# V in 8 KB runs, two batches interleaved over the partitions, and all weights loaded in pairs of slots: a decode kernel of two attention and two GLU layers

## The chip, the cores and the metric

The kernel runs on one core of a Trainium2 chip. The metric is the device time of one execution in microseconds (us). Before the change it is 189 us. With one core there are no others to compare a run with, so runs are called fast unless they lie over 1.5% above the fastest of their kernel. In the profiles PE is TensorE (matrix multiplication) and PEld its loading of weights, DVE VectorE, ACT ScalarE, POOL GpSimd; SPq is the queue of the SyncEngine, which issues all loads here; L372 is a line of the kernel; a landing is the moment at which a load is complete.

## The reference

Four layers in turn (attention, GLU, attention, GLU with the same weights), one new token for each of four batches, bf16.

```python
def attention(x, k_cache, v_cache, wq, wo):      # x: 4 x 1 x 512
    W = 2048                                      # the last 2048 of 8192 keys
    q = (x @ wq)                                  # 32 query heads of 128; 8 kv heads, each shared by 4
    scores = q . k[:, :, -W:, :] * 128 ** -0.5
    o = softmax(scores) . v[:, :, -W:, :]
    return o @ wo                                 # 4096 -> 512
def glu(x, w_gate, w_up, w_down):                 # 512 -> 1792 -> 512
    return (sigmoid(x @ w_gate) * (x @ w_up)) @ w_down

x = x + attention(layernorm(x), ...)
x = x + glu(layernorm(x), ...)
x = x + attention(layernorm(x), ...)
x = x + glu(layernorm(x), ...)
```

There is almost no arithmetic per byte. K and V windows are 16.8 MB each, `wq` and `wo` 4.2 MB each, the three GLU weights 5.5 MB together.

## The kernel before

SBUF holds one arena of 50 slots of 512 KB (4 KB on each of 128 partitions). K takes 32 slots and stays, transposed in place, for both attentions. The other 18 slots are a pool through which everything else streams, in one fixed order, from one load queue (the SyncEngine). `wo` stays after its first load. So do the last three V slots (`KEEP_V`), which the second attention, going through the heads backwards, uses first. Everything else is loaded twice.

V is one load of 512 KB per batch and head, 16 keys (4 KB, contiguous in memory) on a partition:

```python
def kv_d(cache, b, h):
    return cache[b, h, SK - W:SK, :].rearrange("(p j) d -> p (j d)", p=128)

def load_kv(name, cache, b, h):
    loads.append((name, lambda s: dma(str(name), slot_ap(s), kv_d(cache, b, h), w=[("slot", s)])))
# [cut] load_cols: 512 KB of wq, 448 KB of w_gate or w_up; load_rows: 512 KB of wo or w_down
```

A slot goes back to the pool when its last reader is emitted, and the next load in order is put on the queue with a wait on that reader:

```python
def done(name):
    pool.release(where.pop(name))
# [cut]
for gi, (h, b) in enumerate(pairs):               # P.V of one head: 4 batches
    s = need(("V", h, b))
    # [cut] 16 matmuls with 128 x 128 weights taken from the slot
    if (h, b) not in keep:
        done(("V", h, b))
        fill()
```

P leaves softmax with the keys in the free dimension; a matmul with a permutation matrix and a 32 x 32 block transpose turn the keys onto the partitions:

```python
P.op("tensor", "pp" + tag, ..., lambda pe: pe.matmul(ps[:, PB, :], perm[:, :], prow[:, :], start=True, stop=True), ...)
P.op("scalar", "pc" + tag, ...)   # copy back to SBUF
P.op("vector", "pt" + tag, ...)   # 32 x 32 blocks transposed
```

## Time and profile before

| | before |
|---|---|
| time, median | 188.96 us at first, 189.06 us with the run beside the changed kernel |
| span of the profiled run | 187.5 us |
| bytes loaded | 72.37 MB in 122 loads |
| free slots while GLU 1 starts | 7 (18 less 8 of `wo` and 3 of V) |

First some lines of the page: the busy share of the DMA engines and what they moved in 40 equal slices, the count of packets, the head of the chain of waits, and the loads of V and K (count, KB each, median us from issue to landing).

```profile
span 187.5 us, 4426 instructions
...
DMA  4999999999999999999999999999999999999990
GB/s 167 421 421 428 425 407 396 426 383 418 404 395 425 384 415 408 397 421 393 396 402 385 410 408 337 368 410 395 409 408 407 405 409 406 407 409 404 405 371 11
DMA packets 20532, 72.65 MB, mean 387 GB/s; under 512 B 1944, under 2 KB 6048, under 8 KB 17952
...
DMA 38%; SPq 28%; PE 19%; DVE 7%; ACT 3%; issue 3%; ACTq 0%
...
arena<-in_A_v_cache_dram SPq DMA_DIRECT2D x61, 512.0 KB, 14.8
arena<-in_A_k_cache_dram SPq DMA_DIRECT2D x16, 1024.0 KB, 14.8
```

The DMA engines are full from the second slice to the last but one (9 tenths or more in each). What counts is how fast bytes pass, and whether the queue ever runs thin: see 337 and 368 in slices 25 and 26. The stretches view gives the same by time. Its last three columns are the TensorE clock granted, the mean busy share of the 16 DMA engines (packet durations over 16 x the stretch), and GB/s.

```profile
core 0: us, PE busy (x) PEld busy (x) DVE busy (x) ACT busy (x) POOL busy (x), PEclk, DMA share, GB/s
...
20.00:25.00 5.00, 2.02 (x16) 0.38 (x16) 4.91 (x6) 0.20 (x1) 0.00 (x0) 1.00 1.01 423
110.00:115.00 5.00, 3.08 (x26) 0.99 (x26) 1.35 (x6) 1.03 (x5) 0.00 (x0) 0.50 1.00 382
115.00:120.00 5.00, 1.85 (x30) 0.86 (x31) 0.86 (x2) 0.13 (x1) 0.00 (x0) 0.50 0.98 329
120.00:125.00 5.00, 2.07 (x46) 1.76 (x47) 1.26 (x8) 0.41 (x2) 0.00 (x0) 0.50 1.03 411
...
145.00:150.00 5.00, 4.69 (x116) 3.03 (x113) 2.08 (x8) 2.16 (x7) 0.76 (x4) 1.00 1.03 406
155.00:160.00 5.00, 4.71 (x103) 2.82 (x108) 1.82 (x6) 1.68 (x4) 1.13 (x6) 1.00 1.02 406
180.00:185.00 5.00, 2.64 (x63) 2.02 (x60) 1.04 (x3) 0.00 (x0) 0.00 (x0) 0.50 0.52 205
```

At 20 to 25 us only 8 KB packets (K) flow, at 145 to 160 us only 4 KB packets (V).

The waits of the load queue (for whom, us in total, times, longest) show the thin place. The queue stood 7.7 us before GLU 1's first matmuls (L845) gave slots back:

```profile
SPq L372 <- PE ps L755: 18.7, 13, 2.7
SPq L372 <- DVE prow L943: 14.3, 1, 14.3
SPq L372 <- PE ps L845: 9.8, 6, 7.7
```

### The profile page before, as it was taken

Reading aid. Unit: us, or ns where it says so; the run is one execution under the profiler, and the core shown is the slowest. Engines: PE = TensorE matmul, PEld = TensorE weight load, DVE = VectorE, ACT = ScalarE, POOL = GpSimd, SP = SyncE. Lnnn points to the kernel's source line nnn. Section 1 sums busy time; section 2 is a strip of 40 time slices with the busy share of each in tenths; the row PEclk is TensorE's granted clock in tenths of the full one; section 3 lists DMA queues with packets and bytes.
Section 4 is the critical chain, followed back from the end, with each engine's and each line's share of the span. In section 5 each row is a group of like instructions: output and inputs, shape, how many; then the busy total and the mean of one; then the engine's idle time right before and its main releaser. Section 6 shows DMA issues by size and latency. Waiting matters only on the chain.

```text
span 187.5 us, 4426 instructions
## 1 busy us (share of the span) xinstructions
PE 97.6 (52%) x1906; PEld 56.1 (30%) x1920; DVE 86.3 (46%) x215; ACT 32.7 (17%) x95; POOL 13.9 (7%) x73
## 2 busy tenths in 40 slices
PE   0532405456517163270734446344999999775643
PEld 0101002312404033040334331311255555474222
DVE  6109999267583755738510031122484443321211
ACT  2000021213303003020020001000363333210110
POOL 3000000101101001010010000000021111110000
PEclk9999996667857555576675555555799969955555
DMA  4999999999999999999999999999999999999990
GB/s 167 421 421 428 425 407 396 426 383 418 404 395 425 384 415 408 397 421 393 396 402 385 410 408 337 368 410 395 409 408 407 405 409 406 407 409 404 405 371 11
DMA packets 20532, 72.65 MB, mean 387 GB/s; under 512 B 1944, under 2 KB 6048, under 8 KB 17952
## 3 DMA queue, kind: packets, MB, share of 16 engines
q1 hardware_dynamic: 20512, 72.37, 97.9%
q8 instruction: 15, 0.25, 0.5%
q14 instruction: 5, 0.04, 0.1%
HBM read 72.36 MB, written 0.00 MB: 386 GB/s over the span
## 4 chain that ended last, share of the span: by engine, by line
DMA 38%; SPq 28%; PE 19%; DVE 7%; ACT 3%; issue 3%; ACTq 0%
SPq L372 28%; DMA arena<-in_A_k_cache_dram 16%; DMA arena<-in_B_w_down_dram 11%; PE ps L689 11%; DMA arena<-in_A_v_cache_dram 6%; DMA arena<-in_A_wq_dram 5%; PE ps L755 4%; DVE arena L669 3%; ACT prow L706 2%; DVE nmax L697 2%; ACT qbd L656 1%; PE ps L785 1%; PE ps L845 1%; PE ps L877 1%; DVE qbd L653 1%
## 5 line engine op out<-in xcount | busy, mean ns | idle before, releaser
L689 PE MATMUL ps<-arena,qbd 128*16 128x512 bf16 x256 | 32.3, 632 | 29.0 <-DVE arena L669 21.6
L755 PE MATMUL ps<-ebuf,arena 128*128 128x4 bf16 x1024 | 32.0, 166 | 14.9 <-DMA arena<-in_A_v_cache_dram 9.7
L669 DVE STREAM_TRANSPOSE arena<-arena 128x1024 f32<-128x1024 f32 x32 | 38.0, 1220 | 2.7 <-DMA arena<-in_A_k_cache_dram 2.6
L755 PEld LDWEIGHTS ps<-ebuf,arena 128*128 128x128 bf16 x1024 | 29.7, 100 | 18.8 <-DMA arena<-in_A_v_cache_dram 11.9
L697 DVE TENSOR_REDUCE nmax<-ps 128x1 f32<-128x512 f32 x16 | 11.0, 687 | 16.5 <-PE ps L689 16.4
L689 PEld LDWEIGHTS ps<-arena,qbd 128*16 128x16 bf16 x256 | 6.5, 99 | 40.4 <-DVE arena L669 22.1
L767 DVE TENSOR_TENSOR onb<-ps,rinv 128x16 bf16<-128x16 f32 x16 | 3.1, 195 | 31.0 <-PE ps L755 31.0
L706 ACT ACTIVATE prow<-ps,nmax 128x512 bf16<-128x512 f32 x16 | 11.0, 687 | 36.1 <-DVE nmax L703 16.4
L656 ACT CAST qbd<-ps 32x64 bf16<-32x64 f32 x32 | 6.5, 204 | 56.3 <-DVE qbd L653 36.7
L725 POOL CAST s<-psm 128x1 bf16<-128x1 f32 x16 | 3.0, 186 | 144.8 <-ACT prow L706 144.8
L615 PE MATMUL ps<-arena,xn 128*4 128x512 bf16 x64 | 8.3, 588 | 9.2 <-DMA arena<-in_A_wq_dram 6.3
L785 PE MATMUL ps<-onb,arena 128*128 128x4 bf16 x256 | 9.1, 165 | 4.4 <-issue 2.3
L717 ACT CAST prow<-ps 128x512 bf16<-128x512 f32 x16 | 9.4, 585 | 9.4 <-PE ps L755 7.7
L721 DVE STREAM_TRANSPOSE ebuf<-prow 128x256 f32<-128x256 f32 x16 | 7.0, 439 | 7.5 <-ACT prow L717 7.4
L845 PE MATMUL ps<-arena,xn 128*4 128x448 bf16 x64 | 7.2, 555 | 5.6 <-DVE xn L593 2.9
L785 PEld LDWEIGHTS ps<-onb,arena 128*128 128x128 bf16 x256 | 8.0, 100 | 3.7 <-issue 3.3
L653 DVE CAST qbd<-ps 32x64 bf16<-32x64 f32 x32 | 6.7, 209 | 4.7 <-ACT qbd L656 2.5
L623 DVE STREAM_TRANSPOSE ebuf<-ps 128x512 f32<-128x512 f32 x4 | 2.9, 714 | 10.2 <-PE ps L615 10.1
L735 PE MATMUL ps<-sel_b,s 128*128 128x16 bf16 x48 | 3.7, 175 | 7.2 <-POOL s L729 5.6
L582 ACT ACTIVATE lnv<-lnv 128x4 f32<-128x4 f32 x4 | 0.8, 205 | 37.6 <-DVE lnv L579 37.6
L877 PE MATMUL ps<-hT,arena 128*128 128x4 bf16 x112 | 4.3, 167 | 5.0 <-DMA arena<-in_B_w_down_dram 3.7
L852 DVE STREAM_TRANSPOSE ebuf<-ps 128x448 f32<-128x448 f32 x4 | 2.6, 650 | 9.2 <-PE ps L845 9.2
(55 smaller groups left out, 58.1 us busy)
## 6 DMA issues: line engine op xcount, KB each, us to landing
arena<-in_A_v_cache_dram SPq DMA_DIRECT2D x61, 512.0 KB, 14.8
arena<-in_A_k_cache_dram SPq DMA_DIRECT2D x16, 1024.0 KB, 14.8
arena<-in_A_wq_dram SPq DMA_DIRECT2D x4, 1024.0 KB, 7.9
arena<-in_A_wo_dram SPq DMA_DIRECT2D x8, 512.0 KB, 15.5
arena<-in_A_wq_dram SPq DMA_DIRECT2D x8, 512.0 KB, 8.3
arena<-in_B_w_gate_dram SPq DMA_DIRECT2D x8, 448.0 KB, 13.7
arena<-in_B_w_up_dram SPq DMA_DIRECT2D x8, 448.0 KB, 13.6
arena<-in_B_w_down_dram SPq DMA_DIRECT2D x6, 512.0 KB, 7.1
```

The source lines that it names most:

```text
L372: o = P.op("sync", name, 0.0, lambda e, dst=dst, src=src: e.dma_start(dst, src), r=r, w=w, dma_bytes=nbytes, dma_rate=tm[rate])
L615: last = pe.matmul(ps[32 * hh:32 * hh + NB, qb, :], xn[:, c * NB:(c + 1) * NB], slot_ap(s)[:, hh * 512:(hh + 1) * 512], start=(c == 0), st ...
L653: P.op("vector", "qe%s_%d" % (tag, a), c_dve(64), lambda v, dst=dst, src=src: v.tensor_copy(dst, src), r=rd, w=[("q", k2, a)], banks=(rb,))
L656: P.op("scalar", "qe%s_%d" % (tag, a), c_act(64), lambda s_, dst=dst, src=src: s_.copy(dst, src), r=rd, w=[("q", k2, a)], banks=(rb,))
L669: P.op("vector", "T%d_%d" % (h, t), c_dve(1024), lambda v, v32=v32: v.transpose(v32, v32), r=[("slot", 4 * h + t)], w=[("slot", 4 * h + t)])
L689: last = pe.matmul(ps[32 * gi:32 * gi + NR, bank, :], qbd[:, q0:q0 + NR], kt[:, cp // 2, cp % 2, b % 2, :, :], start=(cp == 0), stop=(cp = ...
L697: lambda v: v.tensor_reduce(nmax[:, k2:k2 + 1], ps[:, bank, :], AXX, ALU.max),
L706: lambda a: a.activation(prow[:, :].rearrange("p (m x t) -> p m x t", x=16, t=2), ps[:, bank, :].rearrange("p (m t x) -> p m x t", x=16, t ...
L717: P.op("scalar", "pc" + tag, c_act(512), lambda a: a.copy(prow[:, :].rearrange("p (m y t) -> p m y t", y=2, t=2), ps[:, PB, :].rearrange(" ...
L755: last = pe.matmul(ps[:, ob, gi * REP:(gi + 1) * REP], src[:, j * 128:(j + 1) * 128], ev[:, j % 2, j // 2, gi * REP:(gi + 1) * REP], start ...
L785: last = pe.matmul(ps[:, wb, c * nb:(c + 1) * nb], slot_ap(s)[:, r_ * D + c * 128:r_ * D + (c + 1) * 128], ov[:, o0:o0 + nb], start=(first ...
L845: last = pe.matmul(ps[32 * g:32 * g + NB, SB[n], 0:NF], xn[:, c * NB:(c + 1) * NB], slot_ap(s)[:, g * NF:(g + 1) * NF], start=(c == 0), st ...
```

## The change

The intent is larger runs and fewer, larger loads. V gets K's layout: one load of 1 MB brings two batches, partition 2p from one batch and 2p+1 from the other, with 32 keys (8 KB) each. So P has to come out of the turn masked: each P.V matmul takes the P columns of two batches, and the rows of the other batch's partitions must be zero. The permutation matrix now does this, in four matmuls of 256 columns. All weights are loaded in pairs of slots (1 MB, or 7/8 of it). The pool deals in pairs, so one V pair is kept in place of three slots. That costs an extra 0.52 MB of loads. `w_down` also gets 8 KB (and 6 KB) runs; `wq`'s second load, `wo`, `w_gate` and `w_up` keep their runs of 4, 1 and 3.5 KB.

```diff
-    KEEP_V = cfg.get("KEEP_V", 3)
+    KEEP_V = cfg.get("KEEP_V", 1)
-    FCC = SLOT // D
+    FCC = 2 * SLOT // D
-        pool.free = list(range(4 * HKV, NS))
+        pool.free = list(range(4 * HKV, NS, 2))
         def done(name):
-            pool.release(where.pop(name))
+            left[name] -= 1
+            if left[name] == 0:
+                pool.release(where.pop(name))
+                fill()
+        def pair_d(cache, h, bp):
+            return cache[2 * bp:2 * bp + 2, h, SK - W:SK, :].rearrange("b (p j) d -> p b (j d)", p=64)
+        def load_v(h, bp, k, n_use):
+            load(("V", h, bp, k), n_use, "bw_8k", (2 * SLOT, pair_d(A_v, h, bp), True))
+        def load_wo(hh):
+            load(("wo", hh), 4, "bw_1k", (2 * SLOT, wo_d[:, hh * 2 * REP:(hh + 1) * 2 * REP, :], False))
 # [cut] wq, w_gate, w_up, w_down likewise; q copied once to SBUF; bank numbers
-                 lambda pe: pe.matmul(ps[:, PB, :], perm[:, :], prow[:, :], start=True, stop=True),
+                for jh in range(2):
+                    for i in range(2):
+                        last = pe.matmul(ps[:, PBS[i], 0:256], perm[64 * i:64 * i + 64, jh * 128:(jh + 1) * 128],
+                                         prow[64 * i:64 * i + 64, jh * 256:(jh + 1) * 256], start=(jh == 0), stop=(jh == 1))
-                    for j in range(NJ):
-                        last = pe.matmul(ps[:, ob, gi * REP:(gi + 1) * REP], src[:, j * 128:(j + 1) * 128],
-                                         ev[:, j % 2, j // 2, gi * REP:(gi + 1) * REP], start=(j == 0), stop=(j == NJ - 1))
+                    for j in range(2 * NJ):
+                        x0 = j // 16 * 16 + bp * 8
+                        last = pe.matmul(ps[:, ob, bp * 8:bp * 8 + 8], src[:, j * 128:(j + 1) * 128],
+                                         ev[:, j % 2, j % 16 // 2, x0:x0 + 8], start=(j == 0), stop=(j == 2 * NJ - 1))
 # [cut]
```

## The prediction

> **What bounds the kernel now: the load queue.** The slice table shows the 16 DMA engines 90% busy or more in all slices but the first and last: 72.65 MB, 387 GB/s over the 187.5 us span. The chain of waits agrees: DMA 38%, the load queue's own waits (SPq) 28%. Compute has slack: in the chain the last `w_down` load is issued at 169.2 us and lands 14.3 us later, so that much is queued that no longer depends on compute. A few us of PE, DVE or ACT in either attention should be worth nothing; packet time and gaps in the queue count.
>
> **Packets, from the trace's packet records.** 9600 of 4 KB, mean 165.4 ns; 2560 of 8 KB, mean 317.0 ns. Two 4 KB packets take 331 ns, 4.2% over one of 8 KB. The stretches table agrees: 421 to 433 GB/s at 5 to 25 us (8 KB only), 406 to 410 at 135 to 165 us (V only, 4 KB). [...]
>
> **What changes (estimates from these durations).**
> - V: 61 loads of 512 KB (7808 packets, 80.7 us of 16 engines) become 31 of 1 MB (3968 packets of 8 KB, 78.6 us): -2.1 us. This includes the extra half MB (+1.2 us), as one pair (two slots) is kept in place of three slots.
> - `w_down` in 8 and 6 KB runs: 9.3 to about 8.9 us, -0.4 us.
> - Second `wq`, `wo`, `w_gate`, `w_up`: same runs, fewer loads. Completion packets (1944 of 4 B, 9.5 ns) fall as 123 issues become about 73: -0.5 us.
> - Tail: 24 matmuls follow the last `w_down` landing in place of 8 (16 took 0.59 us): +0.4 us.
> - Turn: four 256-column matmuls in place of one of 512 (389 ns), an ACT copy per q half, q copied from SBUF: tenths of a us per head, hidden under DMA.
> - Middle (GLU 1, q projection 2): the queue runs thin here. The last `w_up` load is issued only at 112.5 us, after 7.7 us blocked on the first `w_gate` matmuls (waits of the queue), with about 0.6 MB in flight by the packets' count; at 113 to 119 us only about 300 GB/s flow, about 1.2 us lost. After: four free pairs for seven slots, 3.67 MB queued before GLU 1 for 3.2 MB (+1.1 us of cover), but a pair comes free only after two chunks (+0.4 us), and PV's last tile is 32 matmuls (+0.6 us). I expect the dip to stay, 0 to 1 us smaller.
>
> Sum: -2.1 -0.4 -0.5 +0.4 = -2.6 us, nearly all on the critical path, since the queue is the path.
>
> **Predicted: 186.4 us, range 184.6 to 188.6.** Faster by over 2%: 0.2; within 2%: 0.76; slower: 0.04.
>
> **What would show it.** V-only stretch of attention 2 at 420 to 428 GB/s in place of 407, its 8 KB packets at 310 to 317 ns; about 73 issues; 72.9 MB in all; about 393 GB/s over the span; the dip after GLU 1 still there; last `w_down` landing to the end 3.5 to 4.5 us.
>
> **What would make it wrong.** 8 KB V packets slow when mixed with `wo` and K or when two batches are read at once; coarser slots starve the queue elsewhere (end of attention 1, start of attention 2, where K pairs come free); the dip after GLU 1 vanishes (1 us faster) or doubles; compute in attention 2 (4.6 us per head, against about 4.9 us of loads per head after) becomes the limit if the turn costs more than it seems.

For 113 to 119 us of before the stretches view gives 327 GB/s, where the text says about 300. Its completion packets are the 4 B packets, 16 of them to each load of the arena (1944 before, 1144 after).

## The result, and the profile after

| | before | after |
|---|---|---|
| time, median | 189.06 us | 188.39 us (188.0 to 188.6) |
| ratio | | 0.9964, 95% interval 0.9943 to 0.9985 |
| the same with five rounds more (run r_after) | 188.99 us | 188.60 us; 0.9973, 0.9945 to 1.0002 |
| span of the profiled run | 187.5 us | 186.3 us |
| loads, bytes | 122, 72.37 MB | 72, 72.89 MB |

A ratio is the mean time of one kernel's fast runs over the mean of the other's of the same rounds, so it isn't quite the ratio of the medians. The gain is 0.4 to 0.7 us, where 2.6 us had been forecast; the second interval reaches 1, so the gain is hardly clear of the noise, and by the 2% measure both pairs count as the same. The median lies just under the top of the range given. The two profiled runs differ by more (1.2 us): that of after was the fastest of its first four runs, that of before (189.24 us) was above all of its own.

The same lines of the page for the kernel after:

```profile
span 186.3 us, 4459 instructions
...
DMA  5999999999999999999999999999999999999980
GB/s 164 419 426 426 424 410 391 415 420 417 407 390 422 417 422 402 396 422 420 387 403 415 407 404 381 394 398 420 422 413 422 413 419 422 420 411 401 413 327 6
DMA packets 15379, 73.17 MB, mean 393 GB/s; under 512 B 1144, under 2 KB 5248, under 8 KB 8576
...
DMA 52%; PE 24%; SPq 17%; DVE 3%; ACT 1%; issue 1%
...
arena<-in_A_v_cache_dram SPq DMA_DIRECT2D x31, 1024.0 KB, 17.0
```

And its stretches, and waits of the load queue:

```profile
core 0: us, PE busy (x) PEld busy (x) DVE busy (x) ACT busy (x) POOL busy (x), PEclk, DMA share, GB/s
...
20.00:25.00 5.00, 2.07 (x16) 0.43 (x16) 4.94 (x7) 0.48 (x2) 0.00 (x0) 1.00 1.02 424
110.00:115.00 5.00, 2.58 (x24) 0.52 (x24) 1.18 (x5) 1.16 (x5) 0.00 (x0) 0.50 1.02 378
115.00:120.00 5.00, 2.02 (x43) 1.13 (x44) 0.87 (x2) 0.00 (x0) 0.00 (x0) 0.50 1.01 413
120.00:125.00 5.00, 2.33 (x34) 1.25 (x34) 1.25 (x8) 0.41 (x2) 0.00 (x0) 0.50 1.01 380
...
145.00:150.00 5.00, 4.51 (x111) 2.67 (x103) 1.96 (x9) 1.85 (x5) 0.76 (x4) 0.98 1.01 416
155.00:160.00 5.00, 4.98 (x114) 2.66 (x103) 1.82 (x6) 1.36 (x3) 0.76 (x4) 1.00 1.01 416
180.00:185.00 5.00, 2.40 (x60) 1.95 (x60) 0.79 (x3) 0.00 (x0) 0.00 (x0) 0.50 0.17 71
```

```profile
SPq L381 <- PE ps L660: 35.3, 2, 18.5
SPq L381 <- DVE prow L909: 17.8, 1, 17.8
SPq L381 <- PE ps L733: 17.6, 9, 4.7
SPq L381 <- PE ps L757: 16.0, 3, 9.0
SPq L381 <- PE ps L592: 10.4, 4, 3.7
SPq L381 <- PE ps L813: 10.2, 4, 7.0
```

The V-only stretch of attention 2 went from 406 to 416 GB/s in the two windows shown (forecast: 420 to 428); over all of 135 to 165 us it went from 408 to 418, fetches of instructions included. The dip at 115 to 120 us went from 329 to 413 GB/s, but at 120 to 125 us after is lower than before, so over 110 to 125 us the mean rose from 374 to 390 only. More us of the queue are now spent waiting for slots (115 in place of 60, by the L381 and L372 lines of this view), but these are waits of the issuer: the DMA share is 0.99 or more in each 5 us from 5 to 180 us, and the span is 1.2 us shorter.

The clearest account is by bytes, because both kernels load the same things in the same order. From the trace's packet records I took when the bytes of each stage had all moved; each cell is the length of the stage in us. The last four columns are runs told below.

| stage (MB) | before | after | v_4k_runs | before_keep2 | after_keep2 | tail_and_7k |
|---|---|---|---|---|---|---|
| attention 1 after `wq`: K, `wo`, V (37.8) | 93.2 | 92.0 | 93.1 | 93.1 | 92.1 | 92.1 |
| GLU 1 (5.5) | 14.8 | 13.9 | 13.8 | 13.6 | 15.2 | 13.7 |
| second `wq` (4.2) | 10.5 | 10.6 | 11.1 | 11.1 | 11.0 | 10.2 |
| second V | 37.6 (15.2) | 37.8 (15.7) | 38.9 (15.7) | 38.8 (15.7) | 37.0 (14.7) | 37.8 (15.7) |
| GLU 2 (5.5) | 14.6 | 14.6 | 15.0 | 15.9 | 14.3 | 14.4 |
| from the last byte to the end | 3.8 | 4.3 | 4.1 | 3.9 | 4.2 | 4.1 |

So longer runs win 1.2 us in attention 1 (v_4k_runs, the changed kernel with V in 4 KB runs, is back at 93.1). In attention 2 the 2.9% higher rate is spent on the extra half MB. GLU 1 wins 0.9 us and the tail loses 0.4 us.

### The profile page after: what moved, and what is told of

Same layout as the page of the kernel before. It is cut to its first block, busy times and chain, and to the rows that moved or that the text cites. A ratio compares the mean times of both kernels' runs of the same rounds, so it can differ in the third digit from the quotient of the medians.

```text
span 186.3 us, 4459 instructions
## 1 busy us (share of the span) xinstructions
PE 101.0 (54%) x1968; PEld 55.4 (30%) x1968; DVE 84.5 (45%) x214; ACT 35.5 (19%) x99; POOL 14.6 (8%) x76
## 2 busy tenths in 40 slices
DMA packets 15379, 73.17 MB, mean 393 GB/s; under 512 B 1144, under 2 KB 5248, under 8 KB 8576
## 3 DMA queue, kind: packets, MB, share of 16 engines
q1 hardware_dynamic: 15360, 72.89, 97.1%
## 4 chain that ended last, share of the span: by engine, by line
DMA 52%; PE 24%; SPq 17%; DVE 3%; ACT 1%; issue 1%
DMA arena<-in_A_v_cache_dram 33%; SPq L381 17%; PE ps L660 11%; DMA arena<-in_B_w_down_dram 9%; PE ps L733 7%; DMA arena<-in_B_w_up_dram 6%; DMA arena<-in_A_wq_dram 5%; PE ps L757 2%; PE ps L689 2%; ACT prow L677 1%; PE ps L592 1%; DVE nmax L668 1%; PE ps L712 1%; PE ps L813 1%; PE ps L846 0%
## 5 line engine op out<-in xcount | busy, mean ns | idle before, releaser
L733 PE MATMUL ps<-ebuf,arena 128*128 128x8 bf16 x1024 | 30.8, 167 | 30.1 <-DMA arena<-in_A_v_cache_dram 26.8
L660 PE MATMUL ps<-arena,qbd 128*16 128x512 bf16 x256 | 32.3, 629 | 15.9 <-DVE qbd L631 8.1
L733 PEld LDWEIGHTS ps<-ebuf,arena 128*128 128x128 bf16 x1024 | 28.6, 100 | 36.8 <-DMA arena<-in_A_v_cache_dram 32.9
L677 ACT ACTIVATE prow<-ps,nmax 128x512 bf16<-128x512 f32 x16 | 11.0, 687 | 37.6 <-DVE nmax L674 25.0
L634 ACT COPY qbd<-qrep 32x64 bf16<-32x64 bf16 x32 | 7.7, 242 | 41.2 <-PE ps L660 40.7
L702 POOL CAST s<-psm 128x1 bf16<-128x1 f32 x16 | 3.0, 188 | 142.9 <-ACT prow L677 142.9
L689 PE MATMUL ps<-prow,perm 64*128 64x256 bf16 x64 | 6.8, 296 | 3.0 <-ACT prow L677 2.7
L600 DVE STREAM_TRANSPOSE ebuf<-ps 128x512 f32<-128x512 f32 x4 | 2.9, 715 | 10.5 <-PE ps L592 10.4
L846 PE MATMUL ps<-hT,arena 128*128 128x4 bf16 x112 | 3.6, 167 | 4.8 <-DMA arena<-in_B_w_down_dram 4.8
L631 DVE COPY qbd<-qrep 32x64 bf16<-32x64 bf16 x32 | 5.3, 165 | 1.5 <-ACT qrep L620 0.9
```

The source lines that it names most:

```text
L634: P.op("scalar", "qe%s_%d" % (tag, a), c_act(64), lambda s_, dst=dst, src=src: s_.copy(dst, src), r=rd, w=[("q", k2, a)])
L660: last = pe.matmul(ps[32 * gi:32 * gi + NR, bank, :], qbd[:, q0:q0 + NR], kt[:, cp // 2, cp % 2, b % 2, :, :], start=(cp == 0), stop=(cp = ...
L677: lambda a: a.activation(prow[:, :].rearrange("p (m x t) -> p m x t", x=16, t=2), ps[:, bank, :].rearrange("p (m t x) -> p m x t", x=16, t ...
L689: last = pe.matmul(ps[:, PBS[i], 0:256], perm[64 * i:64 * i + 64, jh * 128:(jh + 1) * 128], prow[64 * i:64 * i + 64, jh * 256:(jh + 1) * 2 ...
L733: last = pe.matmul(ps[:, ob, bp * 8:bp * 8 + 8], src[:, j * 128:(j + 1) * 128], ev[:, j % 2, j % 16 // 2, x0:x0 + 8], start=(j == 0), stop ...
```

## The experiments

Two theories of the missing 2 us stood at first. The prediction counted every packet at its mean duration (165.4 ns for 4 KB, 317.0 ns for 8 KB). The rival was that an engine pays a fixed time per packet plus a rate per byte. In the packet records of before and after, packets of 1, 2, 3.5, 4, 6 and 8 KB most often took 46, 84, 140, 159, 234 and 309 ns: a line of 8 to 9 ns plus 27.3 bytes per ns. By it two 4 KB packets take 2.9% more time than one of 8 KB; by the means it is 331 over 317 ns, 4.4% (the prediction's 4.2% is the same difference as a share of 331). A third theory came later: that lost time in one place is given back in another.

### Closer times: r_after, v_4k_runs, after_keep2, before_keep2 (one chip, five rounds)

**r_after** is the changed kernel unedited.

> The changed kernel once more, for a closer time. Theory of the prediction (a packet costs its mean duration, 165.4 ns for 4 KB and 317.0 ns for 8 KB): 2.6 us below before, ratio 0.986. Theory of a fixed cost per packet (most 1, 2, 3.5, 4, 6 and 8 KB packets took 46, 84, 140, 159, 234 and 309 ns, which is about 9 ns plus 27.3 bytes per ns): V saves 3840 packets x 9 ns / 16 = 2.2 us and pays 1.2 us for the extra half MB, w_down saves 0.3, completion packets 0.45, the tail costs 0.4; 1.3 us below before, ratio 0.993. The first four runs gave 0.9964, 0.7 us; if that holds, some 0.6 us is still missing from the second theory.

Measured: 188.60 us, ratio 0.9973 (0.9945 to 1.0002). Both theories of the size were too hopeful.

**v_4k_runs** takes away V's run length, and with it the size of V's loads (512 KB again), which stream1 below shows to be worth nothing (409.5 and 409.4 GB/s):

```diff
+                if name[0] == "V":
+                    for i in range(2):
+                        dma(str(name) + "ab"[i], slot_ap(s + i), src[:, :, i * SLOT:(i + 1) * SLOT],
+                            w=[("slot", s + i)], rate="bw_4k")
+                    return
                 dma(str(name), dst, src, w=tok(s), rate=rate)
```

> The changed kernel with every V pair loaded as two loads of 512 KB in 4 KB runs into the same places; all else as after. Theory of the means: 3968 more packets, 3.4 us, and 31 more completions, 0.3 us: 3.7 us over after (2.0%). Theory of the fixed cost: 3968 x 9 ns / 16 = 2.2 us and 0.3 us: 2.5 us over after (1.3%). Rival, that the run length gains nothing in this kernel because the queue waits for something else: under 1 us over after.

Measured: 190.61 us, ratio 1.0091 (1.0056 to 1.0126) to before, so 1.0091 / 0.9973 = 1.012 of after: 2.2 us (the means of the fast runs differ by 2.3 us, give or take 0.6). That is near the fixed cost (2.5 us) and far from the means (3.7 us). The run length does pay, but a third less than forecast. Its stretches:

```profile
140.00:145.00 5.00, 4.91 (x127) 3.05 (x124) 2.59 (x10) 2.10 (x7) 0.76 (x4) 1.00 1.03 411
145.00:150.00 5.00, 4.61 (x105) 2.71 (x101) 2.03 (x8) 2.39 (x7) 0.76 (x4) 0.66 1.03 408
```

The share of 1.03 is that of before again, and the rate nearly (411 and 408 GB/s; before 406 to 410).

**before_keep2** adds the half MB alone, to the kernel before:

```diff
-    KEEP_V = cfg.get("KEEP_V", 3)
+    KEEP_V = cfg.get("KEEP_V", 2)
```

> The kernel before with two V slots kept in place of three: 0.52 MB more to load, 62 loads of V, and eight free slots in place of seven at GLU 1. If bytes set the time: 1.3 us over before (ratio 1.007). If the dip after GLU 1 cost the kernel before its full 1.2 us and shrinks with the eighth slot: only 0.3 to 0.8 us over.

Measured: 190.97 us, ratio 1.0092 (1.0063 to 1.0121): 1.7 us more, not less than the 1.3 us of the bytes. Yet the dip is gone, as the eighth slot should make it:

```profile
115.00:120.00 5.00, 2.24 (x40) 1.20 (x40) 0.87 (x2) 0.13 (x1) 0.00 (x0) 0.50 1.02 406
...
180.00:185.00 5.00, 2.24 (x40) 1.20 (x40) 0.87 (x2) 0.01 (x1) 0.00 (x0) 0.50 0.62 246
```

GLU 1 is 1.2 us shorter than in before, and GLU 2 is 1.3 us longer (table). Filling the dip won nothing in the end in this run. This is what the third theory is about.

The two last runs also close the sum. before_keep2 and v_4k_runs load the same bytes, with V in 4 KB runs in both; one has before's slots, turn and weights, the other has after's. They take the same time (1.0092 and 1.0091; their means differ by 0.0 us, give or take 0.6). So of the change, everything but V's run length and the half MB is worth nothing together, as far as these runs can tell: +1.7 us and -2.2 us make up the result of -0.5 us.

**after_keep2** keeps two V pairs in the changed kernel (`KEEP_V` 2).

> The changed kernel with two V pairs kept in place of one: 1.05 MB less to load, 2.5 us at 416 GB/s, but three free pairs in place of four while GLU 1 starts. If bytes alone set the time: 2.5 us below after. If the queue runs dry again before GLU 1 (2.75 MB of cover, 6.7 us, against some 8 to 9 us until the first pair comes free and its load flows): the dip costs 1.5 to 2.5 us of it, so 0 to 1 us below after, and the trace shows a deep dip at 110 to 115 us.

Measured: 188.76 us, ratio 0.9973 (0.9933 to 1.0013), the same as r_after, as expected if the queue ran dry. 1.05 MB less gained nothing, since three free pairs don't cover the start of GLU 1, and the queue runs thin once more at the start of attention 2 (135 to 140 us):

```profile
105.00:110.00 5.00, 2.20 (x50) 1.94 (x50) 1.09 (x7) 0.00 (x0) 0.00 (x0) 0.50 1.03 408
110.00:115.00 5.00, 2.58 (x24) 0.51 (x24) 1.01 (x4) 1.16 (x5) 0.00 (x0) 0.50 0.72 249
115.00:120.00 5.00, 1.82 (x40) 1.01 (x40) 0.87 (x2) 0.00 (x0) 0.00 (x0) 0.50 1.02 425
...
135.00:140.00 5.00, 4.26 (x70) 1.52 (x63) 3.71 (x13) 3.67 (x10) 1.56 (x8) 0.93 0.77 280
```

Here the DMA share itself falls, to 0.72 and 0.77: engines stood idle. In the table GLU 1 is 1.3 us longer than in after, and the second V only 0.8 us shorter, though it has 1.05 MB less.

### The rates by themselves: stream1

A kernel of loads alone, with a wrong result: seven stretches of 16.8 MB through the same arena, no compute. The edit takes out all operations but the loads and puts these in:

```python
def phase_a():  # 4 KB runs, 512 KB loads
    for h in range(HKV):
        for b in range(NB):
            s = take(1)
            dma(arena[:, s * SLOT:(s + 1) * SLOT], win(b, h).rearrange("(p j) d -> p (j d)", p=128), [("slot", s)])
# b: the 1 MB pairs of the change; c: each pair in two loads of 64 partitions; d: 4 KB runs, 1 MB loads;
# e: 8 KB runs, 1 MB loads, 1 MB of contiguous source
for ph in (phase_b, phase_a, phase_d, phase_c, phase_e, phase_a, phase_b):
    ph()
```

> Loads alone, no compute, a wrong result on purpose: seven stretches of 16.8 MB, in order B A D C E A B. A: 4 KB runs in 512 KB loads (V of before). B: 8 KB runs in 1 MB pairs of two batches (V of after). C: 8 KB runs in 512 KB loads (each pair in two halves of the partitions). D: 4 KB runs in 1 MB loads. E: 8 KB runs in contiguous 1 MB loads. Theory of the fixed cost per packet: A and D at 412 GB/s (159 ns), B, C and E at 424 (309 ns), so run length alone matters, 2.9%. Theory of the means: A and D near 396 to 408, B, C, E near 414 to 425, over 4% apart. If reading two batches at once costs, B is below E; if load size counts, D is above A and B above C. In the kernels V-only stretches ran at 405 and 416; if the loads alone reach 412 and 424, the missing 1.8% is due to the work beside them and hits both alike.

The page's slices, each 8 us, show the seven stretches (B, A, D, then C, E, A, B):

```profile
GB/s 286 425 423 423 421 409 410 409 409 411 408 409 412 409 408 314 228 217 225 226 219 225 224 227 245 422 423 422 423 413 410 410 410 409 415 421 422 422 422 315
```

Inside the stretches (B, A, D, C, E, A, B) the share of the DMA engines and the rate are:

```profile
core 0: us, POOL busy (x), PEclk, DMA share, GB/s
10.00:40.00 30.00, 0.00 (x0) 1.00 1.01 424
47.00:80.00 33.00, 0.00 (x0) 1.00 1.03 409
88.00:120.00 32.00, 0.00 (x0) 1.00 1.03 410
135.00:190.00 55.00, 0.00 (x0) 1.00 1.02 223
204.00:236.00 32.00, 0.00 (x0) 1.00 1.01 422
244.00:276.00 32.00, 0.00 (x0) 1.00 1.03 410
285.00:316.00 31.00, 0.00 (x0) 1.00 1.01 422
```

And by the packet records (to about 0.5 GB/s, by where a stretch is cut):

| form | GB/s | 16 x size / mean duration, GB/s |
|---|---|---|
| A, 4 KB runs, 512 KB loads | 409.5 and 409.6 | 401.6 |
| D, 4 KB runs, 1 MB loads | 409.4 | 400.6 |
| B, 8 KB runs, 1 MB pairs | 424.3 and 421.7 | 419.8 and 418.0 |
| E, 8 KB runs, 1 MB contiguous | 421.7 | 417.8 |
| C, 8 KB runs, 64 partitions a load | 222.7 | 221.0 |

Among the forms over all 128 partitions (A, B, D, E) run length alone counts, by 3.0 to 3.6%; the rates lie near those of the fixed cost (412 and 424). In the kernels the second V passes 1.4% slower than here with either run length (404.0 GB/s in v_4k_runs, 416.2 in after). Half as many loads gain nothing (A and D: 409.5 and 409.4 GB/s). Two batches at once cost nothing (B and E: 421.7 to 424.3 and 421.7 GB/s). And the last column is the mistake of the prediction in the open: the DMA share is 1.01 to 1.03 in all stretches, yet means of durations would put A 2% too low and B only 1% too low. The recorded times of an engine's packets overlap (share over 1), so a mean duration is not the time that a packet costs, and small packets overlap by more (1.03 for 4 KB, 1.01 for 8 KB). C was a surprise: 222.7 GB/s, about half, its 8 KB packets at a mean of 593 ns in place of 312 (B), at a DMA share of 1.02. Each of its loads brings 64 partitions in place of 128; why that halves the rate was not shown.

### The given-back time: stream2, and the landings of all runs

The trace has 16 landings for each load of the arena, with their times; I take them as one for each of the 16 DMA engines. In before, the 16 landings of a load lie within 0.3 us until 31 us. Then one is 1.3 us late (the largest lag goes from 0.29 to 1.62 us), and stays so for all loads that follow; then a second, and so on. The steps fall on the fetches of instructions, which are the packets of the queue that the profile calls instruction, q8: 16 KB each, 15 of them in before and 15 in after, the first at 31.4 and 34.2 us (smaller steps, of 0.5 to 0.8 us, fall on the few 8 KB packets of a second instruction queue, q14). The largest lag of the last engine against the first, in us:

| | end of attention 1 | end of GLU 1 | last load |
|---|---|---|---|
| before | 1.87 | 0.90 | 2.47 |
| after | 2.02 | 1.44 | 2.71 |
| before_keep2 | 1.89 | 1.89 | 4.38 |
| after_keep2 | 1.84 | 0.48 | 1.77 |

In a dip the engines that are ahead run dry and those behind catch up (in after_keep2, with the share at 0.72, the lag fell from 1.84 to 0.48 us). What uses a load waits for its last landing (in before the last load's came at 184.11 us, and the last eight matmuls started at 184.15 us), so a shallower dip can be paid for later with a longer lag. The traces bear this out in part. From the end of GLU 1 to the last load the lag grew by 1.3 to 1.7 us in nine of the ten traces of whole kernels, so what stood at GLU 1 was still there at the end; only in before_keep2 it grew by 2.5 us. There 1.0 us of the extra lag at the end (4.38 against 2.47) dates from GLU 1, and the other 0.9 us came later, as far as the landings tell by which engine a fetch happened to hit: that of 142.4 us struck one of the two engines that were last already (the largest lag went from 3.0 to 4.2 us), where in before that of 142.9 us struck one near the front, and the largest lag stayed at 2.5 us. By the mean of its 16 landings the last load of before_keep2 came only 0.5 us after that of before (183.5 and 183.0 us), less than the 1.3 us of the bytes: for the mean engine the filled dip did win.

**stream2** tests whether fetches make the lag: form B alone, 67 MB, while PE runs 2048 matmuls that depend on no load (edit against stream1).

```diff
+        for g in range(16):
+            def e_mm(pe):
+                last = None
+                for _ in range(128):
+                    last = pe.matmul(ps[:, 0, 0:4], wt[:, 0:128], wt[:, 128:132], start=True, stop=True)
+                return last
+            P.op("tensor", "mm%d" % g, 8000.0, e_mm, r=[("wt",)], w=[("ps",)], banks=(0,))
-        for ph in (phase_b, phase_a, phase_d, phase_c, phase_e, phase_a, phase_b):
+        for ph in (phase_b, phase_b, phase_b, phase_b):
```

> Loads alone in form B (8 KB runs, 1 MB pairs), 67 MB, a wrong result on purpose, while PE runs 2048 matmuls that depend on no load and so makes the core fetch instructions (about 15 fetches of 16 KB, as in the kernels). In before and after the 16 landings of a load lie within 0.3 us of each other until the first such fetch at 31 and 34 us; then one of them is 1.4 to 1.8 us late, and at each further fetch one more. If a fetch holds up one DMA engine's loads: the same steps here, the spread going from 0.3 to 1.5 us or more, and the total longer than 67.1 MB / 423 GB/s by about the largest lag. If the lag came from the compute or from slot waits: the spread stays at 0.3 us throughout.

Measured: 16 fetches (q8 on the page: 16 packets, 0.26 MB), at 6.9, 13.0, 19.2 us and so on to 100.0 us. The lag over the first landing, sorted, of one load after each of some of them:

```
after  1 fetch:   ... 0.35  0.49  1.77
after  2 fetches: ... 0.49  0.60  1.82  1.83
after  8 fetches: 0 to 0.67 (8 engines)   1.75 to 2.07 (8 engines)
after  9 fetches: ...  2.05  3.38
after 16 fetches: 0 to 0.75 (8 engines)   3.31 to 3.67 (8 engines)
```

Each fetch made one landing, so one engine as counted here, 1.2 to 1.5 us late, and it stayed so to the end of the stream. By the count of late landings the first eight struck eight engines, the next eight the same eight again. In the stream without compute (stream1) there was no fetch in the trace (its page has no line of q8), and the lag of a load in forms A and B stayed at 0.6 to 0.9 us throughout. The last landing came 163.1 us after the first packet, 4.5 us later than 67.1 MB at 423 GB/s; the lag is 3.6 us of that. While the fetches last, V's bytes pass at 416 to 418 GB/s (419 with the fetches' own), after them at 422. So the lag is made by fetches. By these rates, as an estimate, they would also account for V's 416 in the kernel (15.7 MB in 37.8 us) in place of 422 GB/s. The rival, that compute holds attention 2 up (PE is busy up to 5.00 us of 5 there), has against it that the DMA share of after stays at 1.00 or more from 130 to 170 us; it was not tested by a run of its own.

### What is left in tail, slots and runs: tail_split, after_keep0, gu_7k_runs, tail_and_7k (one other chip, five rounds)

**tail_split** loads the very last `w_down` tile of 6 rows as 4 and 2.

```diff
+        def bounds_of(k):
+            return bounds if k == 0 else bounds[:-1] + [(8, 12), (12, 14)]
-            for (a, b) in bounds:
+            for (a, b) in bounds_of(k):
```

> The changed kernel with its very last w_down tile (768 KB, 24 matmuls after its landing) loaded as 512 KB and 256 KB, so that 8 matmuls follow the last landing. If the longer tail (4.27 us after the last byte in place of 3.85 before) is a real 0.4 us of the loss: 0.3 us below after (0.1 us is given back to shorter runs). If not: the same as after.

Measured: 188.08 us, ratio 0.9931 (0.9907 to 0.9955); from last byte to end 3.8 us in place of 4.3. Against after, on another chip, that is 0.3 to 0.8 us; the cleaner pair is gu_7k_runs and tail_and_7k below, which differ by this edit alone: 187.58 and 187.12 us, 0.4 us by the ratios. The tail is as large as predicted.

**after_keep0** keeps no V pair.

> The changed kernel with no V pair kept: 1.05 MB more to load, one more free pair at GLU 1. If bytes alone set the time: 2.5 us over after (1.3%). If what is left of the dip after GLU 1 (397 GB/s over that stretch) costs anything that a fifth pair can win back: 0.3 to 0.8 us less than that, 1.7 to 2.2 over after.

Measured: 190.30 us, ratio 1.0048 (1.0023 to 1.0074), about 1.4 to 1.7 us over after (which ran on another chip). The bytes would be 2.5 us. The fifth pair shortens GLU 1 and the second `wq` from 13.8 and 10.7 us (in r_after) to 13.5 and 10.3 us, so here part of the dip seems to have come back as time. The result lies at the lower edge of what was expected or under it.

**gu_7k_runs** gives `w_gate` and `w_up` runs of 7 KB, with four neighbouring rows of the model dimension on one partition. `x` and all outputs follow this order; `wq` is then also read in neighbouring rows.

```diff
-    wg_d = B_wg.rearrange("(kt p) f -> p kt f", p=128)
+    wg_d = B_wg.rearrange("(p kt) f -> p kt f", p=128)
 # wq and w_up alike; wo and w_down columns, x and the output taken at a step of four:
-    tile_ap(s)[:, o + r_ * D + c * 128:o + r_ * D + (c + 1) * 128],
+    tile_ap(s)[:, o + r_ * D:o + (r_ + 1) * D].rearrange("p (m c) -> p c m", c=NC)[:, c, :],
```

> The changed kernel with the model dimension laid over the partitions in groups of four rows, so that w_gate and w_up come in 7 KB runs in place of 3.5 KB (1024 packets fewer); the weights of wo and w_down are then read at a step of four columns. Fixed cost of 9 ns a packet: 0.6 us below after. Means of durations: near 1 us below. If strided weight loads slow PE in the last GLU or the packets don't merge: the same as after or slower.

Measured: 187.58 us, ratio 0.9904 (0.9881 to 0.9927), about 1.0 to 1.3 us below after. GLU 2 shrank from 14.8 us (in r_after) to 14.3 us and the second `wq` from 10.7 to 10.3 us, so the gain mixes longer runs with another order of `wq`'s rows; the tail grew to 4.7 us, presumably by the strided weights (PE's loads of `w_down` weights took 118 ns in place of 104; in tail_and_7k those of `wo` took 117 in place of 101). The edit isn't a clean test of the fixed cost, only a gain.

**tail_and_7k** is both.

> Both of these together, the best version that the runs so far point to: 0.9 us below after by the fixed cost and the tail, so about 1.5 us below before (ratio 0.992).

Measured: 187.12 us, ratio 0.9883 (0.986 to 0.9906), correct, 2.1 us below before by the medians. It beats both kernels, if by less than 2%.

## Why the prediction was wrong

The mechanism was right: the load queue is the path, V's runs were the gain, the turn's extra work hid (PE rose from 97.6 to 101.0 us busy, but the DMA share stayed at 1.00 or more through attention 2). The sum of 2.6 us was wrong; of its terms:

- **"Two 4 KB packets take 331 ns, 4.2% over one of 8 KB" and the step from it, "-2.1 us" for V: this is the failed step.** It is the sum of a gain and a cost. The gain was forecast at 3.3 us (-2.1 less the +1.2 of the half MB) and measured 2.2 us (v_4k_runs); the rates of stream1 on 32.5 MB give about 2.4 us (2.3 to 2.8). The mean durations were inflated twice: packets overlap, and the mean of the 4 KB packets held those of the thin stretch (173 ns at 108 to 132 us, some over 1 us; without them the mean is 164, not 165.4). The overlap stays when the thin stretch is left out: for V in attention 2 alone (135 to 165 us, before and after) the means, 163.3 and 315.0 ns, still say 3.7%, where the stage rates, 404.5 and 416.2 GB/s, say 2.9%. The cost of the half MB was forecast at 1.2 us; its bytes are 1.3 us at 409.5 GB/s, and it measured 1.7 us, within the interval of 1.2 to 2.3. In place of -2.1 us the two came to -0.5 us.
- **"Completion packets: -0.5 us": nothing.** Loads of 512 KB and of 1 MB pass at the same rate (409.5 and 409.4).
- **"`w_down` -0.4 us": 0.1 us at most, not told from nothing.** From the last landing of V to that of `w_down`, GLU 2 took 13.40 us before and 13.27 us after, but 13.36 us in before_keep2 (4 KB) and 13.34 us in v_4k_runs (8 KB).
- **"Tail +0.4 us": right.** 3.8 to 4.3 us in the traces, 0.4 us by the last pair of runs.
- **"I expect the dip to stay, 0 to 1 us smaller": right as far as it went** (0.9 us), but a smaller dip was taken to be so much gained. before_keep2 shows that it needn't be: without a dip in GLU 1 it lost the same time by the end of GLU 2. By the landings about half of the longer lag at its end is lag that no dip made up; the rest is where its fetches fell.
- **The check by stretches misled.** The 421 to 433 GB/s came from a stretch before the first instruction fetch, set against V late in the kernel. 8 KB packets late in the kernel pass at 416 (after, the second V).

With these sizes the sum is -2.4 + 1.3 - 0.1 + 0.4 = -0.8 us and a dip worth little, against 0.4 to 0.7 us measured. What stays open is the last few tenths: the dip's gain and the lag can't be told apart more finely from single profiles, and a slightly changed program moves its fetches against its loads.

## What to carry to other kernels

When the DMA engines are full, take the worth of a packet size from GB/s in stretches that hold that size alone and lie in the same part of the kernel, or from a stream of loads; don't take it from durations of packets, which overlap (a DMA share over 1.00 tells so; here, at 1.01 to 1.03, the durations said 3.7 to 4.4% and the rates of the second V 2.9%). Price the bytes that a coarser layout adds before its gain per byte: here 0.7% more bytes took back more than half of what 8 KB runs gave. In these runs a dip in the queue was worth filling only as far as the last DMA engine, not the mean one, was waiting in it (before_keep2 won 1.2 us in GLU 1 and lost 1.3 us in GLU 2); look at the landings of a load one by one.
